# Seven experts' tokens: block transposes by VectorE, by quarter of the features, into PSUM instead of SBUF

## The chip, the cores and the metric

The kernel runs on one core of one Trainium2 chip. The metric is the time of one execution on the device in microseconds (us); of several executions the median is taken.

The core has five engines, each with its own queue of instructions that it works through in order: TensorE (PE, with its weight loads PEld), VectorE (DVE), ScalarE (ACT), GpSimd (POOL) and SyncE (SP, which here issues most DMAs). SBUF is the working memory, PSUM the memory that TensorE writes its products to. The other two engines that reach PSUM are VectorE and ScalarE.

## What is computed

Attention in which a query sees only the keys of its own hash bucket (4 batches, 8 heads, 768 positions of 64 features), and then a layer of 8 experts, of which each token takes one:

```python
x = attn_out.transpose(0, 2, 1, 3).reshape(B * S, H * D)   # 3072 tokens x 512 features
logits = x @ w_gate                                         # 512 x 8
expert_idx = argmax(logits, axis=1)
gate_w = softmax(logits)[arange(N), expert_idx]
for e in range(8):                                          # tokens sorted by expert
    h = maximum(x_sorted[lo:hi] @ w1[e], 0.0)               # 512 x 1024
    y_sorted[lo:hi] = h @ w2[e]                             # 1024 x 512
out = gate_w[:, None] * y_sorted[inv_perm]
```

## The kernel before

The first 440 us or so are attention. Its results, rows of tokens, are scattered by expert to a buffer in DRAM, `sorted_rows` (`xs`). The change lies in the second part, the experts.

The experts are worked in the order of their token count. `PH` (L698) lists nine phases `(rank, offset, capacity)`: the first expert in two phases (n = 0 and 1) of 256 tokens each, the seven others in phases n = 2 to 8 with capacities of 456, 432, 408, 396, 384, 372 and 354 tokens. For precision every number is split in two: a high part (a copy rounded to the matmul's type, float32r) and a low part (what the rounding left). A product is then three matmuls for each step of the contraction: high by high, low by high, high by low.

What happens in the main loop (L1157) in phase n:

- `rows(n + 1)` (L703) has SyncE fetch the next expert's tokens. For n + 1 > 1 they come by blocks: in partition 32a + i, `XG[n]` holds for each block g the features 128a to 128a + 127 of the expert's row 32g + i. A feature quarter d is 32 features of each of the four groups a. What is then missing for the layout that TensorE wants (features on partitions) is a transpose of blocks of 32x32.
- `mm1(n, f)` for f = 0 to 7 (L802) is the first layer: 12 matmuls into a PSUM buffer `s` (three of them in turn), in the order of the feature quarters d = 0 to 3 and for each d high, low, high of the tokens `XH`. ScalarE makes the high part of the result with relu (L827), VectorE the low part (L829). After each f, `halves` splits a part of a weight chunk: ScalarE copies (L693), GpSimd subtracts (L694).
- `mm2(n, m)` for m = 0 to 3 (L834) is the second layer. Phases with more than 384 tokens compute features by tokens, and ScalarE evicts (L851); the outputs are turned and weighted in the next phase. Phases with up to 384 tokens (n = 1, 6, 7 and 8) go by `yout` (L853): one output tile of 128 tokens per m, 24 matmuls (L867), evicted by VectorE (L878) and scattered to the output by GpSimd (L880). Phase 1 has two such tiles, phases 6 to 8 have three. After each m follow two `halves`.
- `xts(n + 1, ...)` among these prepares the tokens `XH` of the next phase by `xt` (L739), one feature quarter d at a time. The lists `WHEN` (L1153) and `SOON` (L1154, for n = 1) say where: each entry holds the quarters done inside of `mm2(n, m)` (`mid`) and those after it and its `halves` (`end`). For n > 1: quarter 0 after m = 0, quarter 1 inside and quarter 2 after m = 1, quarter 3 inside m = 2. For n = 1: quarters 0 and 1 inside m = 1, 2 and 3 after it. Inside a tile of `yout`, `mid` comes after half of the tile's matmuls and ahead of its eviction.
- For n + 1 > 1, `blocks` (L731) has done the transposes before: up to four instructions on VectorE, each for 128 tokens and all 512 features' worth of blocks, ahead of `mm2(n, 0)`, into an SBUF tile `XT`. `xt` then takes quarter d out of `XT`: a copy by ScalarE for the high part (L755), a subtraction by VectorE for the low part (L756).
- For n < 2, `xt` has TensorE turn the tokens (L750) into a PSUM tile `t`, of which there are two in turn; copy and subtraction read that tile.

The order in which the program emits instructions is the order in each engine's queue (`manual_schedule`).

Of the kernel before, what the change touches and what calls it, by code (L numbers as in the profile page):

```python
# [7 lines left out]
F32 = mybir.dt.float32  # L8
# [42 lines left out]
def tiles_of(n):  # L51

    return [(o, min(128, n - o)) for o in range(0, n, 128)]
# [3 lines left out]
def lsh_attention_moe(ctx, tc, qk2, v, proj, wg, w1, w1q, w2, out):  # L57
    nc = tc.nc
    const = ctx.enter_context(tc.tile_pool(name="const", bufs=1))
    moe = ctx.enter_context(tc.tile_pool(name="moe", bufs=1))  # L60
    ps = ctx.enter_context(tc.tile_pool(name="ps", bufs=1, space=bass.MemoryType.PSUM))
# [601 lines left out]
    P2 = {}  # L663
# [34 lines left out]
    PH = [(0, 0, EARLY), (0, EARLY, CAPS[0] - EARLY)] + [(r, 0, CAPS[r]) for r in range(1, E)]  # L698
    XG, XI, XT, IX, XH, HH, YT, GT = {}, {}, {}, {}, {}, {}, {}, {}
# [3 lines left out]
    def rows(n):  # L703

        r, o, c = PH[n]
        if n > 1:
            XG[n] = P2["p"].tile([128, 16, 2 * D], F32, name="xg", bufs=2)
            XI[n] = P2["p"].tile([128, 4, 2], F32, name="xi", bufs=2)
            t = len(tiles_of(c))
            x = xsv[bass.ds(EV[r], 1), 0:128 * t]  # L710
            for a in range(4):
                nc.sync.dma_start(XG[n][32 * a:32 * a + 32, :4 * t][:, None],
                                  x[:, :, a * PW + E:a * PW + E + 2 * D].rearrange("o (g i) w -> i o g w", i=32))
            nc.sync.dma_start(XI[n][:, :t][:, None], x[:, :, GC:RW].rearrange("o (j p) w -> p o j w", p=128))
            return
        XG[n] = wk.tile([128, 2, RW], F32, name="xd")
        for j, (i, _) in enumerate(tiles_of(c)):
            nc.sync.dma_start(XG[n][:, j], xsv[bass.ds(EV[r], 1), o + i:o + i + 128].rearrange("o p w -> p (o w)"))

    def tokens(n):  # L720
        r, o, c = PH[n]
        IX[n] = moe.tile([128, 4], I32, name="ix", bufs=3)
        t = len(tiles_of(c))
        x = XI[n][:, :t, 1] if n > 1 else XG[n][:, :t, GC + 1]
        nc.vector.tensor_copy(IX[n][:, :t], x.bitcast(I32))

    def heads(x, d):

        return x[:, d * PW + E:d * PW + E + 2 * D]

    def blocks(n, j):  # L731

        if j == 0:
            XT[n] = P2["p"].tile([128, 4, 512], F32, name="xt")
        if j < len(tiles_of(PH[n][2])):
            nc.vector.transpose(XT[n][:, :, 128 * j:128 * j + 128].rearrange("p c (t i) -> p t c i", i=32),
                                XG[n][:, 4 * j:4 * j + 4].rearrange("p t w -> p (t w)"))

    def xt(n, d):  # L739
        r, o, c = PH[n]  # L740
        if d == 0:
            XH[n] = (moe.tile([128, 2, 4, EARLY], F32R, name="xhe") if n < 2 else
                     P2["p"].tile([128, 2, 4, CAPS[1]], F32R, name="xh"))
        t = len(tiles_of(c))
        if n > 1:
            p = XT[n][:, d]
        else:
            p = ps.tile([128, 512], F32, name="t", bufs=2)
            for j in range(t):
                nc.tensor.transpose(p[:, j * 128:(j + 1) * 128], heads(XG[n][:, j], d), ident)  # L750
        if d == 0:
            GT[n] = moe.tile([128, 4], F32, name="gate", bufs=3)
            nc.vector.tensor_copy(GT[n][:, :t], XI[n][:, :t, 0] if n > 1 else XG[n][:, :t, GC])
            tokens(n)
        nc.scalar.activation(XH[n][:, 0, d, :c], p[:, :c], AF.Copy)  # L755
        nc.vector.tensor_tensor(XH[n][:, 1, d, :c], p[:, :c], XH[n][:, 0, d, :c], op=OP.subtract)  # L756
# [3 lines left out]
    def length(n):  # L760

        r = PH[n][0]
        LEN[n] = nc.values_load(C["ni"][0:1, r:r + 1], engines=[mybir.EngineType.PE], min_val=0, max_val=N)
# [38 lines left out]
    def mm1(n, f):  # L802
        r, o, c = PH[n]
        if f == 0:
            if n == 0:
                HH[n] = [wk.tile([128, 8, EARLY], F32R, name="qk") for _ in range(2)]
            else:
                HH[n] = [P2["p"].tile([128, 8, CAPS[1]], F32R, name=f"hh{i}") for i in range(2)]
        w = CH[4 * r + f // 4]
        x = XH[n]  # L810
        h0, h1 = HH[n]
        fs = slice((f % 4) * 128, (f % 4) * 128 + 128)
        p = ps.tile([128, 512], F32, name="s", bufs=3)

        terms = [(w[:, a, d, fs], x[:, b, d]) for d in range(4) for a, b in ((0, 0), (0, 1), (1, 0))]
        products(n, p, c, terms)
        M1[f] = p, c, h0, h1
        if n:
            relu("u", f)
            relu("d", f)  # L820
# [10 lines left out]
    def by_token(n):  # L831
        return PH[n][2] <= 384
# [20 lines left out]
    def yout(n, j, mid=None):  # L853
        r, o, c = PH[n]
        if j >= len(tiles_of(c)):
            return
        i, pw = tiles_of(c)[j]
        if n + 1 == len(PH) and j + 1 == len(tiles_of(c)):
            youts(n, j, i, pw)
            return  # L860
        p = ps.tile([128, 512], F32, name="s", bufs=3)
        if by_token(n):
            k = 0
            for f in range(8):
                w = CH[4 * r + 2 + f // 4]
                for a, b in ((0, 0), (1, 0), (0, 1)):
                    nc.tensor.matmul(p[:pw], HH[n][b][:, f, i:i + pw], w[:, a, f % 4],  # L867
                                     start=(k == 0), stop=(k == 23))
                    k += 1
                    if k == (12 if n else 20) and mid:  # L870
                        mid()
        else:

            yw = max(pw, min(128, CAPS[1] - i))
            for m in range(4):
                nc.tensor.transpose(p[:yw, m * 128:(m + 1) * 128], YT[n][:, m, i:i + yw], ident)  # L876
        y = (P2["p"] if n else moe).tile([128, DM], F32, name="y" if n else "ye", bufs=3 if n else 2)
        nc.vector.tensor_scalar(y[:pw], p[:pw], GT[n][:pw, j:j + 1], None, op0=OP.mult)  # L878
        nc.gpsimd.memset(C["spacer"], 0.0)
        st = nc.gpsimd.indirect_dma_start(out=out, out_offset=bass.IndirectOffsetOnAxis(ap=IX[n][:pw, j:j + 1], axis=0),  # L880
                                          in_=y[:pw], in_offset=None, bounds_check=N - 1, oob_is_err=False)
        for q in outs:
            tc.declare_no_dep(st.ins, q.ins, reason="rows of other tokens")
        outs.append(st)
# [225 lines left out]
    last = [route(B - 1, (0,)), route(B - 1, (1,))]  # L1110
# [18 lines left out]
    def xts(n, ds):  # L1129
        for d in ds:  # L1130
            xt(n, d)
# [11 lines left out]
    def halves(n, k):  # L1143

        if n < 4 * E:
            chunk_part(n + k // 4, k % 4)
            if k % 2:
                h = 2 * n + k // 2 + 3
                if h < LASTH:
                    raw_load(h // 2, h % 2)  # L1150
# [6 lines left out]
    for n in range(1, len(PH)):  # L1157
        c0 = 4 * (PH[n][0] + 1)
        last = n + 1 == len(PH)
        if not last:  # L1160
            rows(n + 1)
            length(n + 1)
        for f in range(8):
            mm1(n, f)
            if f % 2 and not by_token(n - 1):
                yout(n - 1, f // 2)
            halves(c0, f)
            if 3 <= n < 6:
                for _ in range(2):
                    next(plan, None)  # L1170
        for m in range(4):
            mid, end = ((), ()) if last else (WHEN if n > 1 else SOON)[m]
            if m == 0 and not last:
                for j in range(4):
                    blocks(n + 1, j)
            if not (last and m == 3):
                mm2(n, m, lambda: xts(n + 1, mid))
            halves(c0 + 2, 2 * m)
            halves(c0 + 2, 2 * m + 1)
            xts(n + 1, end)  # L1180
        if n == 6:
            for _ in plan:
                pass
        if n == 7:
            C["n"] = nc.values_load(C["cntn"][0:1, 0:1], min_val=0, max_val=TMAX)
# [4 lines left out]
    with tc.For_i(0, C["n"], 1) as i:  # L1190
# [16 lines left out]
        p = ps.tile([128, 512], F32, name="t", bufs=2)  # L1207
# [5 lines left out]
        for f in range(8):  # L1213
            p = ps.tile([128, 512], F32, name="t", bufs=2)
# [3 lines left out]
        p = ps.tile([128, 512], F32, name="s", bufs=3)  # L1218
# [32 lines left out]
```

## Time and profile before

| | before |
|---|---|
| median of 3 runs | 716.64 us (714.62 to 717.83) |
| profiled execution | 715.64 us |
| its span, first to last instruction | 713.8 us |
| mean granted TensorE clock | 0.994 |
| busy: TensorE, VectorE, ScalarE, GpSimd | 691.8, 491.0, 410.9, 487.6 us |

The profile is one execution. A row of a group of instructions names line, engine, operation, the tile written and the tile read, shapes and count, then busy time and the mean duration of one in ns; after the second bar stands the idle time of the engine ahead of them and what ended it. A row of the timeline names start and duration in us, engine, line, operation, tiles, shapes and count; consecutive ones are merged. A granted clock of 1.00 is 2.4 GHz, one of 0.50 is 1.2 GHz.

### The profile page before, as it was taken

Reading aid. Unit: us, or ns where it says so; the run is one execution under the profiler, and the core shown is the slowest. Engines: PE = TensorE matmul, PEld = TensorE weight load, DVE = VectorE, ACT = ScalarE, POOL = GpSimd, SP = SyncE. Lnnn points to the kernel's source line nnn. Section 1 sums busy time; section 2 is a strip of 40 time slices with the busy share of each in tenths; the row PEclk is TensorE's granted clock in tenths of the full one; section 3 lists DMA queues with packets and bytes.
Section 4 is the critical chain, followed back from the end, with each engine's and each line's share of the span. In section 5 each row is a group of like instructions: output and inputs, shape, how many; then the busy total and the mean of one; then the engine's idle time right before and its main releaser. Section 6 shows DMA issues by size and latency. Waiting matters only on the chain.

```text
span 713.8 us, 13651 instructions
## 1 busy us (share of the span) xinstructions
PE 691.8 (97%) x4539; PEld 560.5 (79%) x4539; DVE 491.0 (69%) x942; ACT 410.9 (58%) x830; POOL 487.6 (68%) x729
## 2 busy tenths in 40 slices
PE   8889999999999999999998999999999999999996
PEld 4677668667766776676666788899999999989895
DVE  7998898889888988898998673424676825232321
ACT  5786678668766876787676633544444444444310
POOL 7766676678777777877785663686666667768522
PEclk8999999999999999999999999999999999999999
DMA  8888779868867677687678247683847474747201
GB/s 324 277 232 234 252 229 289 230 183 233 246 198 213 198 202 226 212 258 185 201 206 234 90 143 217 204 216 120 200 127 199 139 194 139 195 161 202 93 12 40
DMA packets 67775, 138.33 MB, mean 194 GB/s; under 512 B 12883, under 2 KB 29523, under 8 KB 67680
## 3 DMA queue, kind: packets, MB, share of 16 engines
q1 hardware_dynamic: 60848, 120.67, 59.4%
q0 software_dynamic: 6688, 16.35, 6.8%
q8 instruction: 61, 1.00, 0.6%
q14 instruction: 34, 0.28, 0.1%
q10 hardware_dynamic: 144, 0.03, 0.0%
HBM read 75.79 MB, written 26.33 MB: 143 GB/s over the span
## 4 chain that ended last, share of the span: by engine, by line
PE 79%; ACT 10%; issue 6%; DVE 4%; POOL 1%; POOLq 0%; ACTq 0%; DVEq 0%
PE s L769 28%; PE t L411 17%; PE s L867 8%; PE s L309 7%; PE s L311 6%; PE t L349 6%; ACT e L335 5%; DVE m L319 2%; ACT pt L375 2%; PE t L264 2%; PE t L430 2%; ACT bits L277 1%; ACT bits L244 1%; PE s L876 1%; DVE w L389 1%
## 5 line engine op out<-in xcount | busy, mean ns | idle before, releaser
L335 ACT ACTIVATE e<-s,m 128x768 f32<-128x768 f32 x192 | 189.9, 992 | 72.2 <-DVE m L326 36.7
L319 DVE TENSOR_REDUCE m<-s 128x1 f32<-128x768 f32 x192 | 177.6, 946 | 27.9 <-PE s L311 24.0
L694 POOL TENSOR_TENSOR w<-raw,w 128x512 fp32r<-128x512 f32 x112 | 145.2, 1323 | 34.1 <-ACT w L693 33.0
L411 PE MATMUL t<-pt,vt 128*64 128x384 f32 x768 | 130.9, 490 | 1.3 <-ACT e L335 1.3
L769 PE MATMUL s<-xh,w 128*128 128x432 f32 (+11 forms) x672 | 121.9, 338 | 0.0
L769 PEld LDWEIGHTS s<-xh,w 128*128 128x128 f32 x672 | 114.6, 188 | 3.1 <-issue 0.8
L411 PEld LDWEIGHTS t<-pt,vt 128*64 128x64 f32 x768 | 52.5, 137 | 65.1 <-issue 62.5
L829 DVE SCALAR_TENSOR_TENSOR hh<-s,hh 128x256 fp32r<-128x256 f32 (+7 forms) x64 | 35.5, 555 | 95.9 <-ACT hh L827 94.6
L349 PE MATMUL t<-ident,e 128*128 128x128 f32 x612 | 91.0, 276 | 7.8 <-ACT pt L375 4.6
L389 DVE STREAM_TRANSPOSE w<-e 128x768 f32<-128x768 f32 x90 | 84.0, 959 | 9.4 <-ACT e L335 8.6
L349 PEld LDWEIGHTS t<-ident,e 128*128 128x128 f32 x612 | 71.5, 140 | 20.0 <-ACT pt L375 8.3
L827 ACT ACTIVATE hh<-s 128x256 fp32r<-128x256 f32 (+7 forms) x64 | 31.3, 490 | 89.9 <-PE s L769 89.9
L769 PE MATMUL s<-hh,w 128*128 128x432 f32 (+5 forms) x384 | 72.3, 349 | 0.0
L324 POOL TENSOR_SCALAR m<-m 128x1 f32<-128x1 f32 x98 | 22.8, 233 | 70.6 <-DVE m L319 68.4
L693 ACT ACTIVATE w<-raw 128x512 fp32r<-128x512 f32 x112 | 66.7, 623 | 7.4 <-DMA raw<-in_w1q_dram 5.8
L769 PEld LDWEIGHTS s<-hh,w 128*128 128x128 f32 x384 | 69.9, 188 | 1.3
L880 POOL DMA_INDIRECT out_dram<-y,ix x26 | 26.9, 1036 | 58.0 <-DVE y L878 22.9
L375 ACT ACTIVATE pt<-t 128x512 f32<-128x512 f32 (+1 forms) x113 | 63.6, 587 | 3.8 <-PE t L349 3.4
L309 PE MATMUL s<-w 80*128 80x384 f32 x192 | 56.2, 374 | 3.3 <-ACT e L335 2.4
L309 PE MATMUL s<-qk 80*128 80x384 f32 x192 | 57.1, 380 | 1.3 <-ACT e L335 1.0
L867 PE MATMUL s<-w,hh 128*128 128x512 f32 (+1 forms) x240 | 56.4, 394 | 0.0
L867 PEld LDWEIGHTS s<-w,hh 128*128 128x128 f32 (+1 forms) x240 | 44.6, 187 | 10.5
(222 smaller groups left out, 1065.4 us busy)
## 6 DMA issues: line engine op xcount, KB each, us to landing
pt<-w SPq DMA_DIRECT2D x240, 144.0 KB, 3.4
raw<-in_w_dram SPq DMA_DIRECT2D x36, 512.0 KB, 3.9
raw<-in_w1q_dram SPq DMA_DIRECT2D x28, 512.0 KB, 4.9
w<-in_qk_dram SPq DMA_DIRECT2D x14, 768.0 KB, 8.0
xd<-in_qk_dram SPq DMA_DIRECT2D x14, 768.0 KB, 7.3
sorted_rows<-xr SPq DMA_DIRECT2D x8, 1156.0 KB, 12.5
vt<-in_v_dram SPq DMA_DIRECT2D x16, 384.0 KB, 3.0
xg<-sorted_rows SPq DMA_DIRECT2D x16, 256.0 KB, 6.6
```

The source lines that it names most:

```text
L309: nc.tensor.matmul(p[:, a, :HALF], k[0:80, 2, c], k[0:80, 3, n], start=i >= 4, stop=i < 4)
L311: nc.tensor.matmul(p[:, a, :HALF], k[:, 0, c], k[:, 1, n], start=i < 4, stop=i >= 4)
L319: nc.vector.tensor_reduce(m[:, 0:1], p[:, :, :HALF], axis=AX.XY, op=OP.max, negate=True)
L335: nc.scalar.activation(e, p[:, :, :HALF], AF.Exp, bias=m[:, 2:3], scale=m[:, 1:2], accum_out=SM[g, hf][:, t, s:s + 1])
L349: nc.tensor.transpose(p[:, x * 128:(x + 1) * 128], e[w][:, kt // 3, (kt % 3) * 128:(kt % 3) * 128 + 128], ident)
L375: nc.scalar.activation(o, x, AF.Copy)
L389: nc.vector.transpose(d.rearrange("p b k q -> p k b q"), PP.pop(i).rearrange("p a c -> p (a c)"))
L411: nc.tensor.matmul(p[s * 64:(s + 1) * 64, :HALF], VT[g][:, kt, s, :], x, start=(kt == 0), stop=(kt == NT - 1))
L693: nc.scalar.activation(w[:, 0, a], r, AF.Copy)
L694: nc.gpsimd.tensor_tensor(w[:, 1, a], r, w[:, 0, a], op=OP.subtract)
L769: nc.tensor.matmul(p[:, :z], w, x[:, :z], start=first and k == 0, stop=k == len(ts) - 1 and (n < 2 or not first))
L867: nc.tensor.matmul(p[:pw], HH[n][b][:, f, i:i + pw], w[:, a, f % 4], start=(k == 0), stop=(k == 23))
```

## The change

`blocks` and the tile `XT` are gone, and so is its call ahead of `mm2(n, 0)`. For n > 1, `xt(n, d)` now takes one of the two PSUM tiles `t` and has VectorE transpose quarter d of all blocks of 32 tokens that the capacity c reaches into, 32 * ceil(c / 32) columns, from `XG[n]` into it. The copy by ScalarE and the subtraction by VectorE then read the PSUM tile. Phases 0 and 1 stay as they are.

```diff
-    def blocks(n, j):
-
-        if j == 0:
-            XT[n] = P2["p"].tile([128, 4, 512], F32, name="xt")
-        if j < len(tiles_of(PH[n][2])):
-            nc.vector.transpose(XT[n][:, :, 128 * j:128 * j + 128].rearrange("p c (t i) -> p t c i", i=32),
-                                XG[n][:, 4 * j:4 * j + 4].rearrange("p t w -> p (t w)"))
-
     def xt(n, d):
         r, o, c = PH[n]
...
         t = len(tiles_of(c))
+        p = ps.tile([128, 512], F32, name="t", bufs=2)
         if n > 1:
-            p = XT[n][:, d]
-        else:
-            p = ps.tile([128, 512], F32, name="t", bufs=2)
+            b = (c + 31) // 32
+            nc.vector.transpose(p[:, :32 * b].rearrange("p (t i) -> p t i", i=32), XG[n][:, :b, 32 * d:32 * d + 32])
+        else:
             for j in range(t):
                 nc.tensor.transpose(p[:, j * 128:(j + 1) * 128], heads(XG[n][:, j], d), ident)
...
             mid, end = ((), ()) if last else (WHEN if n > 1 else SOON)[m]
-            if m == 0 and not last:
-                for j in range(4):
-                    blocks(n + 1, j)
             if not (last and m == 3):
                 mm2(n, m, lambda: xts(n + 1, mid))
```

## Rows read from the trace of the kernel before

**Rows 1.** The page: busy us, share of the span and instructions of each engine

```profile
PE 691.8 (97%) x4539; PEld 560.5 (79%) x4539; DVE 491.0 (69%) x942; ACT 410.9 (58%) x830; POOL 487.6 (68%) x729
```

**Rows 2.** Busy us by stretch: length, PE, PEld, DVE, ACT, POOL, PEclk, DMA, GB/s

```profile
440.00:675.00 235.00, 235.00 (x1297) 221.69 (x1296) 111.38 (x190) 107.07 (x212) 164.51 (x158) 1.00 0.63 173
675.00:690.00 15.00, 15.00 (x97) 14.81 (x96) 4.45 (x8) 3.27 (x7) 6.34 (x6) 1.00 0.07 15
```

**Rows 3.** Waits of PEld from 440 us on: us in total, times, longest

```profile
PEld s L769 <- issue: 0.8, 3, 0.3
PEld s L769 <- DVE xh L756: 0.4, 1, 0.4
PEld s L769 <- DVE hh L829: 0.2, 1, 0.2
```

**Rows 4.** Groups of instructions by shape, from 430 us on, VectorE and ScalarE

```profile
L736 DVE STREAM_TRANSPOSE xt<-xg 128x512 f32<-128x512 f32 x25 | 15.6, 676 | 0.0
L829 DVE SCALAR_TENSOR_TENSOR hh<-s,hh 128x456 fp32r<-128x456 f32 x8 | 5.1, 633 | 14.8 <-ACT hh L827 14.8
L756 DVE TENSOR_TENSOR xh<-xt,xh 128x432 fp32r<-128x432 f32 x4 | 4.9, 1264 | 4.3 <-ACT xh L755 4.3
L756 DVE TENSOR_TENSOR xh<-xt,xh 128x456 fp32r<-128x456 f32 x4 | 2.3, 626 | 0.0
...
L851 ACT ACTIVATE yt<-s 128x456 f32<-128x456 f32 x4 | 2.2, 553 | 10.2 <-PE s L769 10.2
L755 ACT ACTIVATE xh<-xt 128x456 fp32r<-128x456 f32 x4 | 2.1, 572 | 1.3 <-DVE xt L736 1.3
```

**Rows 5.** Timeline of VectorE around the end of phase 1

```profile
452.43 2.48 DVE L736 STREAM_TRANSPOSE xt<-xg 128x512 f32<-128x512 f32 x4
...
456.24 0.16 DVE L753 COPY gate<-xi 128x4 f32<-128x4 f32 x1
...
461.13 0.75 DVE L878 TENSOR_SCALAR y<-s,gate 128x512 f32<-128x512 f32 x1 [3.58 <-PE s L867]
461.80 1.17 DVE L756 TENSOR_TENSOR xh<-xt,xh 128x456 fp32r<-128x456 f32 x2
```

**Rows 6.** The page: costliest groups of the whole span

```profile
L389 DVE STREAM_TRANSPOSE w<-e 128x768 f32<-128x768 f32 x90 | 84.0, 959 | 9.4 <-ACT e L335 8.6 <-DMA pt<-w 0.7
L769 PEld LDWEIGHTS s<-xh,w 128*128 128x128 f32 x672 | 114.6, 188 | 3.1 <-issue 0.8
```

**Rows 7.** Timeline of ScalarE and GpSimd around the end of phase 1

```profile
454.94 1.06 ACT L755 ACTIVATE xh<-xt 128x456 fp32r<-128x456 f32 x2 [1.28 <-DVE xt L736]
457.90 2.18 ACT L693 ACTIVATE w<-raw 128x512 fp32r<-128x512 f32 x4
...
463.31 13.77 POOL L694 TENSOR_TENSOR w<-raw,w 128x512 fp32r<-128x512 f32 x11
```

**Rows 8.** Timeline of ScalarE and TensorE, second layer of phase 2

```profile
490.47 1.14 ACT L693 ACTIVATE w<-raw 128x512 fp32r<-128x512 f32 x2
...
480.37 19.08 PE L769 MATMUL s<-hh,w 128*128 128x456 f32 x96
499.29 4.88 PE L769 MATMUL s<-xh,w 128*128 128x432 f32 x24
```

**Rows 9.** Timeline of VectorE, TensorE and GpSimd, end of phase 7

```profile
671.02 0.95 DVE L756 TENSOR_TENSOR xh<-xt,xh 128x354 fp32r<-128x354 f32 x2
...
675.73 14.99 PE L769 MATMUL s<-xh,w 128*128 128x354 f32 x96
...
678.32 5.03 POOL L694 TENSOR_TENSOR w<-raw,w 128x512 fp32r<-128x512 f32 x4
```

**Rows 10.** Timeline of PEld, first product of phase 2

```profile
460.70 1.41 PEld L769 LDWEIGHTS s<-xh,w 128*128 128x128 f32 x7
462.47 1.09 PEld L769 LDWEIGHTS s<-xh,w 128*128 128x128 f32 x6 [0.36 <-DVE xh L756]
```

**Rows 11.** Busy us by stretch, as rows 2; the column behind POOL is the granted clock

```profile
10.00:15.00 5.00, 5.00 (x16) 3.32 (x15) 3.22 (x7) 3.22 (x7) 4.71 (x7) 0.50 1.06 379
380.00:382.50 2.50, 1.14 (x7) 0.73 (x5) 2.36 (x7) 1.12 (x3) 2.34 (x4) 1.00 0.98 282
```

## The prediction

> **What bounds the kernel now.** I read the busy table of the page first: TensorE is busy for 97% of the span, no other engine for more than 69% [rows 1]. That is an average over an attention part and an expert part, and the change lies in the expert part alone (phases n = 2 to 8, from about 438 us on), so I cut that part out: in 440 to 675 us TensorE is busy for 235.00 of 235.00 us, and in 675 to 690 us for 15.00 of 15.00 [rows 2]. VectorE is busy there for 111 of 235 us, ScalarE for 107, GpSimd for 165. The list of waits of TensorE's weight loads says how little is left: after 440 us they wait for 1.4 us in all, and only one wait of 0.4 us has anything to do with `xh` [rows 3]. So in this part no microsecond saved on VectorE can shorten the kernel by itself; the most that any edit of VectorE or ScalarE can win is the 0.6 us of [rows 3] that they cause. What it can do is delay TensorE. The question is therefore where the distance between "xh is split" and "TensorE reads xh" is small.
>
> **What is removed.** 25 transposes of 128x512 from SBUF to SBUF, 0.676 us each [rows 4], 16.9 us of VectorE in all, standing in VectorE's queue before the first product of the second layer of phase n (`mm2(n, 0)`). The queue row shows them as one block of four in 2.48 us [rows 5], four us and more ahead of the subtractions that read them.
>
> **What is added.** 28 transposes, four per expert, each of one feature quarter, 32 columns for each started block of 32 tokens: 480 columns for a capacity of 456, then 448, 416, 416, 384, 384, 384. The price of one into SBUF follows from two rows: 512 columns take 0.676 us [rows 4] and 768 take 0.959 us [rows 6], so 1.11 ns a column, and 480 columns take 0.64 us, 384 take 0.53 us. In all 16.0 us, about what is removed. No row of this trace has VectorE write to PSUM. From below I bound it by the spacing of the block of four (2.48/4 = 0.62 us for 512, so 0.58 us for 480); a gain beyond that is excluded, since no uncontended VectorE row here goes faster per column. From above by the dearest rate of a wide VectorE row in this part, the subtraction that takes 1.264 us for 432 columns [rows 4], so 1.40 us. I take 0.64 us, because the same operation over the same columns is the nearest row.
>
> The Trainium skill (VectorE: DVE Perf Modes, section Specifications) speaks against the move: it places VectorE nearer to SBUF and ScalarE nearer to PSUM, without a figure. Rows bear out the half that can be seen: ScalarE needs 0.553 us for 456 columns out of PSUM and 0.572 out of SBUF [rows 4]. By the page the transposes would cost more than 0.64 us and ScalarE's copies 0.02 us less; that is the direction of the first rival below.
>
> **What is moved.** The readers of the transposed tokens now read PSUM. ScalarE's copy of 456 columns then costs 0.55 us, as L851 does from PSUM. VectorE's subtraction costs 0.63 us, as L829 does for 456 columns with one operand in PSUM and one in SBUF, while GpSimd works beside it [rows 4, 7]. The subtraction with both operands in SBUF took about 1.25 us in 16 of its 28 instances (phases 3 to 6, the row of 432 columns stands for them) and 0.63 or less in the other twelve (the row of 456), so VectorE saves about 16 x 0.65 = 10 us. By [rows 2] all of that is off the path: worth nothing.
>
> **The order on the queues** is what counts. Both engines run in the order in which the program emits. Before, all transposes were done before anything of the second layer. Now a quarter is a chain of its own: transpose (VectorE), copy (ScalarE), subtraction (VectorE), and the next quarter's transpose stands behind that subtraction. I went through the phase starts.
>
> Phases 3 to 6 (n + 1): quarters 0, 1 are emitted after the first product, 2, 3 after the second, and nothing on VectorE there waits for TensorE. In phase 2, after ScalarE's eviction of the second product there are two weight copies, done at 491.6 us, then the chain of two quarters (the first transpose is done by then): 2 x (0.53 + 0.6) + 0.6 + 0.04 for each of four handoffs, 3.0 us, so the last split ends near 494.6 us; TensorE starts to read at 499.29 us [rows 8]. Margin nearly 5 us.
>
> Phases 7 and 8: the chain of quarters 2, 3 stands behind the eviction L878 of the last tile but one. From 671.02 us, where the two subtractions stood: 2 x (0.53 + 0.04 + 0.47 + 0.04 + 0.53) less an overlap of 0.08, so 674.2 us; the products begin at 675.73 us and need quarter 3's low part eleventh, 1.5 us later [rows 9]. Margin 3 us; even at 1.40 us for a transpose more than 1 us is left. ScalarE's weight copies behind these move later by some 8 us, but GpSimd reads the last four of them only from 678.3 us on, and the products that need them start when those 96 are done, at 690.7 us.
>
> Phase 2 has no margin. Phase 1 has only two output tiles, so the second half of its chain (quarters 2, 3) stands behind `y(1,1)`, which VectorE evicts when TensorE has done its last matmul of phase 1. Before, only the two subtractions stood there: 461.80 to 462.97 us [rows 5], and TensorE's eighth weight load waited 0.36 us for the first of them, until 462.47 us [rows 10]. Now, from the same 461.80 us: transpose to 462.44; copy 462.47 to 463.02; subtraction 463.06 to 463.69; transpose 463.61 to 464.25; copy 464.28 to 464.83; subtraction 464.87 to 465.50. (Handoffs of 0.03 to 0.04 us and an overlap of 0.08 us as between the rows of [rows 5, 7]: 454.91 to 454.94, 461.88 to 461.80.) The product takes its twelve matmuls quarter by quarter, each quarter high, low, high. So the eleventh needs the second subtraction and can start near 465.57 us. Before, the eighth started at 462.47 and the eleventh three loads of 0.188 us later [rows 6], at 463.03. **The sum: 465.57 - 463.03 = 2.54 us later.** TensorE's queue is in order, so every matmul behind it waits too, and by [rows 2, 3] nothing later is waiting for anything else: no slack takes it back.
>
> Quarters 0, 1 of phase 2 also start later, behind `y(1,0)`, from 456.24 us [rows 5]: their chain ends near 460.0 us (2 x 1.9 less the overlap), needed when TensorE is done with phase 1, near 461 us. That costs nothing. The weight copies emitted among these move later on ScalarE, the last four from 457.90 to about 464.8 us; GpSimd's row of subtractions that starts at 463.31 and reads them shifts by 2 us [rows 7], while the weights are needed in the second layer of phase 2, from 480.37 us on [rows 8], and TensorE shifts by as much. Neither queue has TensorE behind it: the first ScalarE eviction of phase 2 comes some 0.6 us late, and two more product buffers cover it; without them it would cost that 0.6 us. SyncE loses nothing: no DMA is moved.
>
> The profiled execution: 715.64 us with a span of 713.8, so 716.3 span and 718.2 us after. The median of the runs shown is 716.64, 1.0 above it: **719.2 us**, +0.35%.
>
> **Rivals.**
> Transposes into PSUM are dear. Price: two of them lie in the chain of phase 2, so +0.2 us per 0.1 us. It decides from 1.15 us each, when the loss passes 3.6 us; at the bound of 1.40 us the loss is 4.1, and 0.3 more because quarter 1's subtraction pushes `y(1,1)`: 720.2 to 721.0 us. For it: VectorE has no row that writes PSUM. Against: reading PSUM costs VectorE nothing that can be seen (0.633 us against 0.626 [rows 4]). Chance 0.10.
>
> The clock of TensorE falls in the thin stretch. Between 462.5 and 465.6 us only some four matmuls would run. Early in the kernel the granted clock was 0.50 (1.2 GHz) in 10 to 15 us, after TensorE's halting start [rows 11]; were it to stand there for those 5 us of phase 2, dense matmuls would lose 2.5 us more: 721.7 us. Against: with TensorE busy for 1.14 of 2.5 us the granted clock stayed at 1.00 (2.4 GHz) [rows 11]. The Trainium skill (TensorE: Matmul & The Clock Gate, Part 1) has the clock fall when TensorE is idle and return with work; the last row shows a stretch as thin as this one that didn't do it. Chance 0.05.
>
> No stall. If the transposes of quarters 2, 3 ran in VectorE's idle 3.58 us before `y(1,1)`, the chain would start at 457.6 us and cost nothing: 716.6 us, at best 716.3 without the old wait. Against: the old subtractions were ready then too and still ran behind `y(1,1)` [rows 5]. The same time results if the change only moves work about. Chance 0.10.
>
> Faster. Weight splits on GpSimd no longer compete with 16 subtractions of 1.25 us; were they on the path, up to 10 us could be won: 706.6 to 713 us. [Rows 2, 3] speak against it. Chance 0.03.
>
> **How the numbers follow.** My forecast has 0.72: 2.4 to 3.4 us, so 719.0 to 720.0, and some 0.8 us each way for a median of few runs that lie between 714.62 and 717.83. A measurement of this kernel can tell about 0.5%, 3.6 us, from no change. Slower by more: 0.09 out of the forecast, 0.10 and 0.05 from the first two rivals: 0.24. Faster by more: 0.03. Within: 0.73. The range runs from the no-stall case to the dear transposes, 716.8 to 721.4; outside are the clock, the gain and the edges.
>
> **What would show it.** In the profile after, a wait of the weight loads of L769 for VectorE or ScalarE (`xh`) of 2 to 3.5 us in all near 462 to 466 us, once and at no other phase start; transposes near 0.64 us at 480 columns; subtractions of 0.52 to 0.63 us in every phase. A transpose above 1.1 us, a granted clock under 1.00 after 462 us, or waits before phases 3 to 8 would prove me wrong.

## The result

| | before | after |
|---|---|---|
| median | 716.21 us (16 runs, 713.13 to 718.35) | 720.66 us (16 runs, 717.72 to 722.93) |
| ratio | | 1.0059, 95% interval 1.0044 to 1.0074 |
| profiled execution, its span | 715.64, 713.8 us | 721.83, 720.1 us |

The change costs 4.2 us (3.2 to 5.3), 0.6%. 2.54 us were forecast.

The busy table and the stretch of [rows 2], after:

```profile
PE 697.6 (97%) x4539; PEld 564.0 (78%) x4539; DVE 484.5 (67%) x945; ACT 411.4 (57%) x830; POOL 483.8 (67%) x729
```

```profile
440.00:675.00 235.00, 232.85 (x1282) 219.74 (x1283) 102.98 (x190) 104.08 (x207) 157.49 (x154) 0.99 0.63 173
464.00:467.00 3.00, 1.43 (x6) 0.56 (x4) 1.76 (x4) 1.23 (x3) 2.85 (x3) 1.00 0.44 163
467.00:468.00 1.00, 0.80 (x3) 0.48 (x4) 0.54 (x1) 1.00 (x3) 1.00 (x2) 0.91 0.00 0
468.00:471.00 3.00, 3.00 (x10) 2.64 (x9) 0.63 (x1) 1.91 (x4) 3.00 (x3) 0.50 0.57 180
471.00:472.00 1.00, 1.00 (x6) 0.94 (x5) 0.00 (x0) 0.00 (x0) 1.00 (x2) 0.88 0.63 123
```

(Columns as in [rows 2].) VectorE, ScalarE and GpSimd all work less than before in 440 to 675 us, and it gained nothing. TensorE, which had no gap there, now has 2.15 us of them, 1.8 within 464 to 468 us. And behind that thin stretch the granted clock stands at 0.50, 1.2 GHz, from about 467.8 to 471.2 us (0.91 and 0.88 are the means of the slices in which it falls and rises); before, it was 1.00 throughout.

The waits of the weight loads from 440 us on answer to [rows 3]:

```profile
PEld s L762 <- ACT xh L748: 2.1, 2, 1.2
PEld s L762 <- issue: 1.2, 4, 0.6
PEld s L762 <- DVE xh L749: 1.0, 2, 0.5
```

L762 is L769 of before. The 0.4 us of waiting for `xh` has become 3.0 us, in four waits. The timeline of the weight loads, against [rows 10], shows that all four stand in the first product of phase 2:

```profile
462.66 1.21 PEld L762 LDWEIGHTS s<-xh,w 128*128 128x128 f32 x6
465.08 0.19 PEld L762 LDWEIGHTS s<-xh,w 128*128 128x128 f32 x1 [1.20 <-ACT xh L748]
465.74 0.30 PEld L762 LDWEIGHTS s<-xh,w 128*128 128x128 f32 x2 [0.48 <-DVE xh L749]
466.93 0.19 PEld L762 LDWEIGHTS s<-xh,w 128*128 128x128 f32 x1 [0.88 <-ACT xh L748]
467.59 0.69 PEld L762 LDWEIGHTS s<-xh,w 128*128 128x128 f32 x3 [0.48 <-DVE xh L749]
468.46 17.58 PEld L762 LDWEIGHTS s<-xh,w 128*128 128x128 f32 x83 [0.18 <-issue]
486.05 0.19 PEld L762 LDWEIGHTS s<-hh,w 128*128 128x128 f32 x1
486.80 3.25 PEld L762 LDWEIGHTS s<-hh,w 128*128 128x128 f32 x17 [0.56 <-issue]
```

Six loads run at once (quarters 0 and 1), then each of quarters 2 and 3 waits twice: for its high part, then for its low part. Before, the same 83 loads that now take 17.58 us took 16.26:

```profile
463.91 16.26 PEld L769 LDWEIGHTS s<-xh,w 128*128 128x128 f32 x83 [0.34 <-issue]
```

VectorE's timeline, against [rows 5], has the chain that the loads wait for:

```profile
463.09 0.75 DVE L871 TENSOR_SCALAR y<-s,gate 128x512 f32<-128x512 f32 x1 [1.10 <-PE s L860]
463.76 0.68 DVE L740 STREAM_TRANSPOSE t<-xg 128x480 f32<-128x480 f32 x1
465.06 0.63 DVE L749 TENSOR_TENSOR xh<-t,xh 128x456 fp32r<-128x456 f32 x1 [0.62 <-ACT xh L748]
465.61 0.68 DVE L740 STREAM_TRANSPOSE t<-xg 128x480 f32<-128x480 f32 x1
466.91 0.63 DVE L749 TENSOR_TENSOR xh<-t,xh 128x456 fp32r<-128x456 f32 x1 [0.62 <-ACT xh L748]
```

The spans differ by 6.3 us, the medians by 4.5. Of the 6.3, 2.0 lie ahead of anything that the change touches: phase 2's first matmul starts at 462.89 us instead of 460.93, and over the profiles below, whose attention part is the same, that moment lies anywhere between 459.5 and 462.9. So for parts of the loss I compare from that matmul to the end of the last one. Before: 707.52 - 460.93 = 246.59 us. After, from 462.89 to 713.88 us: 713.88 - 462.89 = 250.99 us, 4.40 more. The terms:

- the chain: first to eleventh load 2.33 us before (460.70 to 463.03), 4.93 after (462.66 to 467.59): **2.60 us**
- the 83 loads behind, which run at the lower clock until 471.2 us: 17.58 - 16.26 = **1.32 us**
- waits named "issue" (TensorE's sequencer, no engine): 0.56 us at 486.80 where there was none, 0.16 less at 468.46: 0.40 us.

Together 4.32 of the 4.40.

### The profile page after: what moved, and what is told of

Read it like the earlier page. It is cut to its first block, busy times and chain, and to the rows that moved or that the text cites. A ratio compares the mean times of both kernels' runs of the same rounds, so it can differ in the third digit from the quotient of the medians.

```text
span 720.1 us, 13648 instructions
## 1 busy us (share of the span) xinstructions
PE 697.6 (97%) x4539; PEld 564.0 (78%) x4539; DVE 484.5 (67%) x945; ACT 411.4 (57%) x830; POOL 483.8 (67%) x729
## 4 chain that ended last, share of the span: by engine, by line
PE 80%; ACT 8%; issue 5%; DVE 4%; POOL 1%; POOLq 0%; ACTq 0%; DVEq 0%
PE s L762 28%; PE t L411 17%; PE s L309 8%; PE s L860 8%; PE s L311 7%; PE t L349 7%; ACT e L335 4%; DVE m L319 2%; PE t L430 2%; PE t L264 2%; ACT pt L375 1%; PE s L869 1%; ACT bits L277 1%; ACT bits L244 1%; DVE w L389 1%
## 5 line engine op out<-in xcount | busy, mean ns | idle before, releaser
L694 POOL TENSOR_TENSOR w<-raw,w 128x512 fp32r<-128x512 f32 x112 | 142.5, 1298 | 41.8 <-ACT w L693 40.7
L762 PE MATMUL s<-xh,w 128*128 128x432 f32 (+11 forms) x672 | 124.0, 341 | 1.8 <-ACT xh L748 1.4
L762 PEld LDWEIGHTS s<-xh,w 128*128 128x128 f32 x672 | 115.8, 190 | 5.8 <-ACT xh L748 2.1
L762 PE MATMUL s<-hh,w 128*128 128x432 f32 (+5 forms) x384 | 72.6, 349 | 0.2 <-issue 0.2
L762 PEld LDWEIGHTS s<-hh,w 128*128 128x128 f32 x384 | 69.9, 188 | 1.8 <-issue 0.6
```

Source lines behind the costliest of these rows:

```text
L694: nc.gpsimd.tensor_tensor(w[:, 1, a], r, w[:, 0, a], op=OP.subtract)
L762: nc.tensor.matmul(p[:, :z], w, x[:, :z], start=first and k == 0, stop=k == len(ts) - 1 and (n < 2 or not first))
```

## Experiments

Three theories compete. Theory A: the whole loss stands at the start of phase 2, a chain behind an eviction plus a fall of TensorE's clock. Theory B: the way through PSUM costs a little in each of the seven phases. Theory C: PSUM is what is dear, not the order. Ratios are to the kernel before, with the 95% interval in brackets.

**Which phase.** Two kernels split the change in halves: `p2_sbuf` has the old transposes for phase 2 alone, `p2_psum` has the new ones for phase 2 alone. The edit in essence, for `p2_psum`, against the changed kernel (the other has the conditions turned; `blocks` stands as before):

```diff
-        p = ps.tile([128, 512], F32, name="t", bufs=2)
-        if n > 1:
+        if n > 2:
+            p = XT[n][:, d]
+        else:
+            p = ps.tile([128, 512], F32, name="t", bufs=2)
+        if n == 2:
...
+            if m == 0 and not last and n + 1 > 2:
+                for j in range(4):
+                    blocks(n + 1, j)
```

> Phase 2's tokens go as before (four wide transposes into SBUF ahead of the second layer of phase 1), those of phases 3 to 8 by quarters into PSUM. Theory A (all of the loss sits at the start of phase 2: 2.6 us of chain plus a fall of TensorE's clock): time as before, 716 us, ratio to before 0.999 to 1.002, no wait of over 0.5 us of the weight loads for xh, granted clock 1.00 from 440 us on. Theory B (the PSUM path costs a little in each of seven phases): 6/7 of the loss stays, 719.5 to 720 us, ratio 1.005.

Measured: 716.07 us, ratio 0.9998 (0.998 to 1.0015).

> The other half: phase 2's tokens by quarters into PSUM, those of phases 3 to 8 as before. Theory A: the whole loss, 720 to 721 us, ratio 1.005 to 1.007, waits of the weight loads for xh of 3.0 us in all at the start of phase 2 and a granted clock of 0.50 for some 3 to 4 us behind them. Theory B: one seventh of the loss, 716.8 us, ratio 1.001.

Measured: 720.06 us, ratio 1.0058 (1.0038 to 1.0077). Theory B is out: six of seven phases through PSUM cost nothing that shows (at most 1.1 us by the interval), the seventh has all of it. The weight loads of `p2_psum` in phase 2, and its clock:

```profile
467.04 0.49 PEld L775 LDWEIGHTS s<-xh,w 128*128 128x128 f32 x3 [0.48 <-DVE xh L762]
467.95 17.77 PEld L775 LDWEIGHTS s<-xh,w 128*128 128x128 f32 x83 [0.42 <-issue]
```

```profile
468.00:471.00 3.00, 3.00 (x9) 2.79 (x10) 0.64 (x1) 1.35 (x3) 3.00 (x4) 0.50 0.59 194
```

Again 2.6 us of chain (first load at 462.11, eleventh at 467.04: 4.93 us), again a clock of 0.50, here at a price of 17.77 - 16.26 = 1.51 us. In `p2_sbuf` the eighth load waits 0.36 us as before and nothing else does.

**Order or memory.** `sbuf_quarter` keeps order and quarters and only changes where a quarter is put:

```diff
-        p = ps.tile([128, 512], F32, name="t", bufs=2)
+        p = P2["p"].tile([128, 512], F32, name="xt", bufs=2) if n > 1 else ps.tile([128, 512], F32, name="t", bufs=2)
```

> Order and quarters as in the changed kernel, but each quarter is transposed into one of two SBUF tiles instead of a PSUM tile. Theory A (the order costs, not the memory): at least the same loss, 720 to 722 us, ratio 1.005 to 1.008; transposes of 480 columns at 0.64 to 0.68 us; subtractions of 1.2 us wherever GpSimd reads SBUF beside them, 0.6 elsewhere; were both subtractions of the chain at the dear price, the chain would be 1.2 us longer. Theory C (writing or reading PSUM is what is dear): time as before, 716 us, and transposes well under 0.6 us.

Measured: 727.14 us (5 runs), ratio 1.0151 (1.0117 to 1.0184). Theory C is out, with a loss beyond what I expected. Its VectorE and GpSimd in the same place:

```profile
464.47 0.67 DVE L740 STREAM_TRANSPOSE xt<-xg 128x480 f32<-128x480 f32 x1
465.79 3.06 DVE L749 TENSOR_TENSOR xh<-xt,xh 128x456 fp32r<-128x456 f32 x1 [0.65 <-ACT xh L748]
468.77 0.67 DVE L740 STREAM_TRANSPOSE xt<-xg 128x480 f32<-128x480 f32 x1
470.09 0.63 DVE L749 TENSOR_TENSOR xh<-xt,xh 128x456 fp32r<-128x456 f32 x1 [0.65 <-ACT xh L748]
...
465.86 2.49 POOL L694 TENSOR_TENSOR w<-raw,w 128x512 fp32r<-128x512 f32 x2
```

A transpose into SBUF is 0.667 us on the mean, into PSUM 0.683: the memory makes 0.02 us. But a subtraction with both operands in SBUF took 3.06 us where two of GpSimd's subtractions stood beside it, and 0.63 us where GpSimd had no such work. (The Trainium skill, SBUF — State Buffer, section Who interferes with whom, has it that a VectorE instruction with two SBUF inputs contends with a GpSimd instruction that reads SBUF, and calls what they share an exclusive lock. The rows agree: GpSimd's two subtractions took 2.49 us, no longer than the 2.57 us of such a pair in the changed kernel, and VectorE's ended 0.50 us after them.) The eleventh load comes 8.74 us after the first here, 6.41 us later than before, and the granted clock stands at 0.50 from about 467.8 to 474.6 us; waits for `xh` before phases 7 and 8 are also part of the loss. So PSUM is the better place for a chain that something waits for: in the order of the change it is worth 720.66 against 727.14 us.

**Moving the chain ahead of the evictions.** `early`:

```diff
-    SOON = (((), ()), ((0, 1), (2, 3)), ((), ()), ((), ()))
+    SOON = (((0, 1), ()), ((2, 3), ()), ((), ()), ((), ()))
```

> The changed kernel with only the place of phase 2's preparation moved: quarters 0 and 1 inside the first output tile of phase 1 instead of the second, quarters 2 and 3 inside the second instead of behind it, so that each pair stands ahead of an eviction instead of behind it. Theory A: the chain of quarters 2 and 3 starts 4.5 us earlier and is done when TensorE begins phase 2; the loss goes, 715.8 to 716.5 us, ratio 0.998 to 1.001, clock 1.00. A rival: the two evictions are now about 1 us later and TensorE waits for their buffers, which leaves 1 us or more of the loss, 717 to 718 us.

Measured: 715.44 us, ratio 1.0001 (0.9982 to 1.002). From phase 2's first matmul to the last one it takes 246.44 us, no weight load waits for `xh`, and the first layer of phase 2 is one piece:

```profile
459.50 19.10 PE L762 MATMUL s<-xh,w 128*128 128x456 f32 x96
```

The delayed evictions cost TensorE nothing that shows. The change's mechanism, all seven experts through PSUM, is thus as fast as before (within 1.4 us by the interval), not faster.

**A shorter chain.** `pair` does both transposes of a pair ahead of its copies and subtractions, in phase 2 (`xt` does the one with k = 0 and the other with k = 1):

```diff
...
     def xts(n, ds):
+        if n == 2:
+            for k in range(2):
+                for d in ds:
+                    xt(n, d, k)
+            return
...
```

> The changed kernel with phase 2's quarters in pairs: both transposes first, then copy and subtraction of the one, copy and subtraction of the other. The second copy no longer waits for the first subtraction. Theory A: the chain behind the eviction is 0.68 + 0.60 + 0.63 + 0.60 us long instead of 3.8, so the eleventh matmul starts some 1.3 us late instead of 2.6; if the clock stays, 717.5 us and a ratio of 1.002; if it falls all the same, 719 us and 1.004.

Measured: 717.62 us, ratio 1.0015 (0.9998 to 1.0033).

```profile
462.39 1.21 PEld L770 LDWEIGHTS s<-xh,w 128*128 128x128 f32 x6
464.80 0.19 PEld L770 LDWEIGHTS s<-xh,w 128*128 128x128 f32 x1 [1.20 <-ACT xh L735]
465.47 1.10 PEld L770 LDWEIGHTS s<-xh,w 128*128 128x128 f32 x6 [0.48 <-DVE xh L736]
467.01 16.27 PEld L770 LDWEIGHTS s<-xh,w 128*128 128x128 f32 x83 [0.45 <-issue]
```

Quarter 3 no longer waits. The eleventh load is the fourth of the row at 465.47, so 466.03: 3.64 us after the first instead of 2.33, the 1.3 us expected. The clock stays at 1.00 and the 83 loads take 16.27 us. From first to last matmul 1.41 us more than before.

**A chain that starts one eviction earlier.** `between` has `SOON = (((), (0, 1)), ((2, 3), ()), ((), ()), ((), ()))`.

> The changed kernel with quarters 0 and 1 of phase 2 behind the first output tile of phase 1 and quarters 2 and 3 inside the second: all four in a row from the first eviction on, ahead of the second. Theory A: four times 1.86 us from 0.7 us after the first eviction's start, so the last subtraction ends 2.9 us after TensorE begins phase 2, where 2.3 us are free: a stall of 0.5 to 0.9 us, clock 1.00, 716.6 us, ratio 1.001. If the order on VectorE doesn't matter: as the changed kernel.

Measured: 717.86 us, ratio 1.0028 (1.0009 to 1.0047).

```profile
464.92 0.19 PEld L762 LDWEIGHTS s<-xh,w 128*128 128x128 f32 x1 [0.61 <-ACT xh L748]
465.59 0.50 PEld L762 LDWEIGHTS s<-xh,w 128*128 128x128 f32 x3 [0.48 <-DVE xh L749]
...
484.54 5.61 PEld L762 LDWEIGHTS s<-hh,w 128*128 128x128 f32 x29 [1.47 <-issue]
```

The stall is the one expected: the eleventh load 3.08 us after the first (462.51), 0.75 later than before. The time lost is 2.0 us (0.6 to 3.4), so the 0.7 expected are at the edge of the interval. In the profile, first to last matmul take 2.46 us more than before, and a wait of 1.47 us named "issue" at the start of the second layer makes most of the difference. Waits of this kind, 0.5 to 1.75 us long, come up at different products in some of the profiles and not in others. Each stands behind the first load of a product, where the program branches on the expert's token count (`products`). What they wait for the profile doesn't show, and I have not found it.

**Is it the clock?** `fill` gives TensorE work in the waits of phase 2's first product, `fill_half` in the last two of them only:

```diff
-    def products(n, p, c, terms):
+    def products(n, p, c, terms, idle=None):
...
             for k, (w, x) in enumerate(ts):
+                if idle is not None and not first:
+                    warmth(idle, {5: 5, 6: 2, 8: 3, 9: 2}.get(k, 0))
...
```

(`warmth` does that many matmuls on constants into `idle`, a product buffer that nobody reads. k counts from the second matmul of the product, so the four entries stand ahead of the seventh, eighth, tenth and eleventh, the ones that wait.)

> The changed kernel, and in the first product of phase 2, ahead of the four matmuls that wait, 5, 2, 3 and 2 matmuls on constants (bfloat16, 128x512, some 0.21 us each) into a product buffer that nobody reads: TensorE works while it waits. Theory A1 (the loss is two things: a chain of 2.6 us, and 1.3 to 1.6 us for a clock that falls because TensorE has little to do in the chain): granted clock 1.00 throughout, the chain stays, 719.0 us, ratio to before 1.0035 to 1.0045. Theory A2 (the clock has nothing to do with how full TensorE is there, or costs nothing): as the changed kernel, ratio 1.0058.

Measured: 720.47 us (6 runs), ratio 1.0063 (1.0038 to 1.0089).

> The same with the constants' matmuls only ahead of the last two waits (3 and 2, some 1.1 us of work). Theory A1: TensorE is busy for 1.1 us more in the thin stretch; either the clock stays at 1.00 and the time is 719.0 us, or it falls as in the changed kernel and the time is 720.4 us; in both cases the time goes with the clock, and the chain of 2.6 us stays.

Measured: 718.74 us, ratio 1.0045 (1.0026 to 1.0065).

The weight loads of `fill`:

```profile
466.27 0.49 PEld L764 LDWEIGHTS s<-xh,w 128*128 128x128 f32 x3 [0.25 <-DVE xh L749]
466.92 16.26 PEld L764 LDWEIGHTS s<-xh,w 128*128 128x128 f32 x83 [0.15 <-issue]
```

The chain is untouched (first load at 461.34, eleventh at 466.27: 4.93 us), the granted clock stays at 1.00, and the 83 loads take 16.26 us, as before the change. `fill_half` has 4.93 us and 16.21, also at 1.00. So in these profiles the 1.3 us are gone with the fall. From first to last matmul `fill` takes 249.71 us, 1.28 less than the changed kernel. `fill_half` takes 250.70, hardly less: without a fall, a wait of 1.75 us named "issue" at 622 us stands in its place. The times don't decide it: `fill`'s interval reaches into both theories' figures, with its ratio nearer to A2's, and `fill_half`'s holds both.

So I repeated the stall at all seven phase starts, without and with the filling. `late_all`:

```diff
-    WHEN = (((), (0,)), ((1,), (2,)), ((3,), ()), ((), ()))
+    WHEN = (((), ()), ((0, 1), ()), ((), ()), ((), (2, 3)))
```

> The changed kernel with quarters 2 and 3 of phases 3 to 8 also put behind the last product of the phase before, so that the stall of phase 2 stands at all seven phase starts. Theory A1: each of the six new stalls costs 2.6 to 2.9 us of chain and, where the clock falls behind it, 1.3 to 1.6 us more: 738 to 748 us, ratio 1.030 to 1.044; falls of the granted clock to 0.50 behind most of the seven starts. If the fall behind phase 2 is an accident of that place, one fall in seven and 737 us.

Measured: 740.33 us (6 runs, 737.76 to 745.44), ratio 1.0352 (1.0306 to 1.0399). `late_fill` has that line and `fill`'s for every phase from 2 on.

> The same with the constants' matmuls (5, 2, 3, 2) ahead of the four waits at each of the seven starts. Theory A1: no fall of the clock at any start, the chains stay: 6 to 10 us less than without them (1.3 to 1.6 us for each fall that is avoided), 735 to 738 us, ratio 1.026 to 1.030. Theory A2 (the clock costs nothing in the time): the same time as without them, within 2 us.

Measured: 738.53 us (6 runs, 737.03 to 739.25), ratio 1.0305 (1.027 to 1.0339). Stretches of `late_all`:

```profile
465.00:469.00 4.00, 3.62 (x16) 2.88 (x17) 1.26 (x2) 3.06 (x7) 4.00 (x4) 1.00 0.38 126
...
509.00:511.00 2.00, 2.00 (x7) 1.88 (x7) 0.61 (x1) 0.96 (x2) 0.97 (x1) 0.50 1.24 184
666.00:668.00 2.00, 2.00 (x8) 1.92 (x8) 0.40 (x2) 0.89 (x2) 2.00 (x3) 0.50 0.18 15
```

Its seven stalls are alike, four waits of 2.6 to 3.0 us in all at each start (none longer than 1.33 us), and the clock fell behind two of them, those of phases 3 and 7, each time for some 3.4 us. Behind phase 2's it did not, though the four waits there (1.20, 0.48, 0.88, 0.48 us) are the very ones behind which it fell in the changed kernel. With the filling it fell behind none of seven. So a stall of this form makes a fall possible, not certain. In time the filling won 1.8 us by the medians and 3.2 by the means (741.6 and 738.4), not the 6 to 10 that I had expected of falls at most starts; the two intervals overlap. Without it the runs spread over 7.7 us, with it over 2.2. The mean granted clock of each execution is on record beside its time: without the filling, the two runs of 745.4 us have 0.976 and the four of 737.8 to 740.4 us have 0.987 to 0.992; with it, all six have 0.989 to 0.992. So the two longest runs did have the lower clock, as falls in a changing number would have it; where in them it was low isn't shown, since only one execution of each kernel has a profile.

## Why the prediction was right, and where it was short

The place, the mechanism and the term that I summed were right. From the same eviction on, VectorE, ScalarE and TensorE did in this order what I had listed, and the eleventh load came 2.60 us late; 2.54 were forecast. Of the pieces, a transpose of 480 columns was 0.683 us, not 0.64: 0.03 of that was in my line through wider transposes (into SBUF it is 0.667), 0.02 in PSUM. Copy and subtraction were as priced. The sign named for this came, too: waits for `xh` of 3.0 us in all, at no other phase start. These rows answer to [rows 4]:

```profile
L740 DVE STREAM_TRANSPOSE t<-xg 128x480 f32<-128x480 f32 x4 | 2.7, 683 | 0.0
L749 DVE TENSOR_TENSOR xh<-t,xh 128x456 fp32r<-128x456 f32 x4 | 2.5, 632 | 2.4 <-ACT xh L748 2.4
L749 DVE TENSOR_TENSOR xh<-t,xh 128x432 fp32r<-128x432 f32 x4 | 2.4, 607 | 7.7 <-ACT xh L748 7.7
...
L748 ACT ACTIVATE xh<-t 128x456 fp32r<-128x456 f32 x4 | 2.2, 551 | 7.7 <-DVE t L740 7.7
```

The subtractions of 432 columns fell from 1.264 to 0.607 us, and that was worth nothing: VectorE's and GpSimd's saved time lies under TensorE, as [rows 2] said. The margins of the other phases held. In phase 8 the last subtraction ends at 680.59 us, 3.1 us ahead of its use (the products begin at 682.08, the eleventh matmul 1.56 later); 3 were forecast. Two readings on the side were not exact, and nothing hangs on them: the old block of transposes ended 1.5 us ahead of the first subtractions that read it (454.91 to 456.38 us; four counts from its start), and one cast in the attention part (128x384 in 0.359 us) does go faster per column, at 0.93 ns, than the 1.21 ns that were to exclude a gain.

What was short is the step on the clock. I had it as a rival, with the right place, 2.5 us of price and a chance of 0.05; it came to pass in the profile of the changed kernel, at 1.3 us, and with it 0.4 us more of waits named "issue", which I had left out. A granted clock under 1.00 after 462 us was among the signs that were to prove me wrong, and on this step it does. The evidence that I set against it was one row, 380 to 382.5 us of [rows 11], in which TensorE was busy for 1.14 of 2.5 us and the clock stayed. The stretch that came out here, 1.43 of 3.0 us in 464 to 467, isn't thinner than that row, and `late_all` shows both outcomes behind the same stall. So does the row itself. In `fill`'s profile the same place of the attention part, with the same wait of 1.36 us for ScalarE, stands at 380 to 382.5 us again, and there the clock fell behind it, from about 382.4 to 385.8 us:

```profile
380.00:382.50 2.50, 1.14 (x6) 0.80 (x6) 2.36 (x7) 1.72 (x3) 2.42 (x3) 0.98 0.93 262
383.00:385.00 2.00, 2.00 (x10) 2.00 (x10) 1.28 (x4) 1.08 (x2) 1.82 (x3) 0.50 0.91 233
```

One row in which nothing happened was no ground for 0.05. Of the nine unfilled stalls of this form in the profiles (one each in the changed kernel and `p2_psum`, seven in `late_all`) four had a fall behind them, so something like a half would have been right, and a forecast of 3 to 4 us. The price was too high because I had the lower clock stand for 5 us; it stood for 3.4.

The first rival, dear transposes into PSUM, is out (0.02 us). The third, no stall, is out: the chain did run behind the eviction. The gain is out. The time lies in the range, and that is in part luck: the 1.5 us by which it exceeds 719.2 come from the clock and the "issue" waits as far as the profile tells, both left outside of the range, and they found room that was there for dear transposes and for scatter. The chance of 0.73 for "within 0.5%" was too high, too: the loss came out at 0.59% (0.44 to 0.74), just beyond that line, where the chain alone would be 0.36%.

What stays open: what those "issue" waits are, and how often the clock falls behind such a stall and so what it is worth on the mean. The mean loss of 4.2 us (3.2 to 5.3) fits the chain with a fall in most executions, or with some falls and some of the "issue" waits. The mean granted clocks of the executions on record give an estimate. They average 0.9912 over the 28 runs of the changed kernel and `p2_psum`, and 0.9927 over the 90 of the kernel before, `p2_sbuf` and `early`; with the stall filled (`fill`, `fill_half`, 15 runs) they average 0.9926. One fall for 3.4 us would take 0.0024 off. The 0.0015 between the first two (standard error 0.0007) would thus be a fall in some three of five executions, worth 0.8 us of the mean loss at 1.3 us each, if nothing else differs between them.

## What to carry to other kernels

When a step that was done in bulk ahead of time is broken up into chains done just in time, go through every place where the chain runs and compare its end with the moment of use: six of seven had some 3 us or more to spare, and the whole loss was in the one where the chain stood behind an eviction that waits for the last matmul. There, emitting the pieces one output tile earlier undid the loss without touching the rest. Savings on engines under a TensorE that never waits were worth nothing here, and a stall of a dense TensorE can cost more than its own length: 2.6 us of chain became 4.4 in the profile. One stretch behind which the clock stayed is no evidence that it will stay the next time.

## What the hardware showed that I had not expected

- After stalls of 2.6 to 3.0 us in four waits, none longer than 1.3 us, with matmuls between them, the granted clock fell from 1.00 to 0.50 (2.4 to 1.2 GHz) for some 3.4 us: behind phase 2's in the changed kernel and in `p2_psum`, behind two of seven in `late_all`, and behind none where TensorE was given other matmuls in the waits. Price of one fall in dense matmuls: 1.3 to 1.5 us.
- The same thin stretch of the attention part (1.14 us of TensorE in 2.5, one wait of 1.36 us) had a fall behind it in `fill`'s profile and none in that of the kernel before.
- VectorE's 32x32 transposes write PSUM at almost the price of SBUF: 0.683 and 0.667 us for 128x480 in float32.
- A VectorE subtraction with both operands in SBUF took 3.06 us beside two GpSimd subtractions and 0.63 us without; with one operand in PSUM it took 0.63 us in either case (`early` has both).
